# Two batches share the converted weights of the first layer, in a new order of its tiles

## The chip, the cores and the metric

The kernel runs on one core of one Trainium2 chip. The metric is the device time of one execution in microseconds (us). TensorE (PE in the profile) does the matmuls, VectorE (DVE) and ScalarE (ACT) the elementwise work, GpSimd (POOL) some small work and some transfers, SyncE (SP) issues most transfers.

## The reference

An attention of 4 batches, 12 heads, 448 positions and 64 columns per head, with q and k normalized, feeds two layers of weights one after the other:

```
q_n, k_n = rmsnorm(q, g_q), rmsnorm(k, g_k)
attn = softmax(q_n @ k_n^T / 8);  x = attn @ v            # 1792 tokens x 768
h = x @ w_in;  g = h * clip(h + 3, 0, 6) / 6;  x = g @ w_out     # 768 -> 2048 -> 768
h = x @ w2_in; g = max(h, 0)^2;                out = g @ w2_out  # 768 -> 2048 -> 768
```

All in float32 at the outside.

## The kernel before

**Numbers.** A float32 operand of the two layers is split into an upper and a lower float16 half. A product of two operands is three float16 matmuls (upper x upper, upper x lower, lower x upper) into one PSUM tile. A moving operand is 128 x 448: 128 features of one batch.

**Weights of the first layer.** `w_in` is cut into 16 input tiles (128 of the 2048 columns, 768 rows: `INS`), `w_out` into 6 output rows of 128 columns, each in three tiles of 6, 5 and 5 blocks of 128 (`OUTS`, 18 tiles). The weights come in as 64-bit words. `convert` (L962) makes a tile ready for its first use: it loads the raw words into `wr`, rebuilds float32 values in `wf` (`words_of`: the sign L944, a scaled word L927 or L931, the low bytes L937, their union L948, the sum of magnitudes L954 or L951), gets a scale for a family of tiles (two input tiles, or the three of an output row) through a small matmul (`scale_of`), and writes the halves into `ws` (upper L998 or L1001, lower L1005). The halves are also stored to memory (`spill`). The batch that uses a tile first has it `fresh`; every later batch loads it again (`again`, L1131), on SyncE's or GpSimd's queue.

**Units.** `units` (L41) lists the work of the first layer as (batch, layer, tile). Before, a batch's 16 input units come first, then the last 6 output units (two rows) of the batch before it, then its own first 12 output units (four rows). The last 6 of the last batch (`LEFT`) come later, among the second layer's work. `unit` (L1192) issues a unit's matmuls (L1217): an input unit takes 6 blocks x 3 = 18 matmuls and needs the batch's six x tiles (one for each pair of heads), an output row takes 16 blocks x 3 = 48 and needs the 16 tiles of g. A finished input unit goes through the gate (L1249 on ScalarE, L1252 on VectorE) into a raw tile `gr`, which is then split into halves `g` by a factor d (upper L1281 or L1284, lower L1287). The factor (`factors`, L1258) needs the magnitudes of all 16 input tiles, so no g can be split before the last input tile is converted. A finished output row goes to `yr` and to memory (`kept`).

**Attention.** `attention` (L630) does one pair of heads of one batch: scores (L755), the row maximum (L764), the exponential (L709), a transpose (on TensorE at L719 for batch 0 and five of batch 1's pairs, by a transposing transfer `pt` for the others) and the product with v (L823, L842), then the halves of x (L859 to L870).

**Second layer.** `sums` (L1040) converts its weights (`wr_in`, `wr_out`, `wq`, `wc`, `spill_i`, `spill_o`); its matmuls are at L1471 (input) and L1561 (output), with operands loaded as `wi` and `wo`.

**What sets the order.** Every piece of work is a `Task` with a key (its due time, in units), one or two engines that may do it with a cost, tasks that it waits for, and the buffers it uses. `Plan.order` (L200) plays this through and writes each engine's instructions out in the order that results; on the chip every engine takes its own list in that order. Keys come from the position of a unit in the list (`pos`), from `STEPS` and `SCALE` for attention, from `FROM`, `EVERY` and `SOON` for the second layer's weights, from `LOOK0` and `LOOK` for the conversions and reloads; two long tables (`LATER`, `EARLIER`) move single tasks and buffers. Buffers come in classes: "H" (x, gr, g, yr and others) has 48, "w" (wf, ws, wc) has 8 (L140).

Of the kernel before, what the change touches and what calls it, by code (L numbers as in the profile page):

```python
# [60 lines left out]
FROM, EVERY, SOON = 80.22859998528665, (4.041588453004579, 3.7237456628771537), 8.562933226270134  # L61
YLEAD = 12.522739408787375
# [8 lines left out]
    (-247.48221047888984, -394.5979975821401, -98.4527970272032, -242.42713432233748, -222.88569014639836, -217.12283909562356),  # L71
    (-59.661346379600985, -85.02395686962647, 7.106072067009842, 16.896302439366927, -24.194647662679873, 15.416178359589999),
    (43.66694725987674, 32.553603037054934, 46.34866310324863, 49.82797377644987, 49.208523452314246, 51.17752208559789),
    (35.30617020359621, 38.97394296166319, 65.5895982637515, 168.80800044783174, 66.02963739277855, 73.89482410210749),
# [1591 lines left out]
```

## Time and profile before

| | |
|---|---|
| runs | 1115.54, 1122.12, 1120.02 us |
| median | 1120.02 us |
| profiled execution | 1112.35 us, of which the span is 1110.6 us |
| mean granted clock of TensorE | 0.989 |
| TensorE matmuls, busy | 1043.4 us (94%), 5957 instructions |
| VectorE, busy | 887.0 us (80%), 1971 instructions |
| ScalarE, busy | 759.5 us (68%), 1527 instructions |
| transfers | 243.00 MB, mean 219 GB/s |

The span runs from the first to the last instruction of the profiled execution. Busy times are sums over the whole span; the stages have different limits. PEclk is the clock that TensorE was granted as a share of 2.4 GHz, and it has two levels, 2.4 and 1.2 GHz, so 0.95 over a stretch means that a tenth of it ran at the lower level.

### The profile page before, as it was taken

The numbers are of one execution on the slowest core, as the hardware profiler recorded it, in microseconds if no ns is written. First come the engines' busy times: TensorE is split into PE (matmuls) and PEld (weight loads), VectorE is DVE, ScalarE is ACT, GpSimd is POOL, SyncE is SP. The second block draws the span as 40 slices with busy tenths as digits, with TensorE's granted clock in tenths as the row PEclk, the third lists the DMA queues.
The fourth block names the chain that finished last, engine by engine and source line by source line (L and its number), as shares of the span: only waits on it lengthen the run. The fifth ranks groups of instructions, "written<-read, shape, count | busy, mean of one in ns | idle before, by whom it ended". The sixth has DMA issues, their size and how long they took to land.

```text
span 1110.6 us, 17566 instructions
## 1 busy us (share of the span) xinstructions
PE 1043.4 (94%) x5957; PEld 526.5 (47%) x5957; DVE 887.0 (80%) x1971; ACT 759.5 (68%) x1527; POOL 129.6 (12%) x225
## 2 busy tenths in 40 slices
PE   1789999899999999999999999989999999999998
PEld 0445544445444444444555445544445555555554
DVE  7999999997899998999388989796799952128930
ACT  2899989996689666877276767686766645555520
POOL 4411311202221223320000000000000000000000
PEclk9899999899999999999999999999999999999999
DMA  9756578599899999997998898797856664434343
GB/s 297 185 163 163 194 217 239 178 259 240 246 260 192 227 266 261 233 237 179 296 333 277 303 324 319 247 282 245 255 172 213 211 200 116 121 102 134 106 155 106
DMA packets 232313, 243.00 MB, mean 219 GB/s; under 512 B 144608, under 2 KB 188128, under 8 KB 232224
## 3 DMA queue, kind: packets, MB, share of 16 engines
q1 hardware_dynamic: 228576, 225.00, 70.5%
q0 software_dynamic: 3648, 16.88, 5.2%
q8 instruction: 47, 0.77, 0.3%
q14 instruction: 42, 0.34, 0.1%
HBM read 162.76 MB, written 45.61 MB: 188 GB/s over the span
## 4 chain that ended last, share of the span: by engine, by line
PE 59%; DVE 16%; DMA 14%; ACT 8%; issue 2%; SPq 1%; POOL 0%; DVEq 0%; ACTq 0%
PE m L1217 21%; PE mo_0A L1561 3%; PE ps_s L755 3%; PE mo_1A L1561 3%; PE mo_2A L1561 3%; PE ps_a L842 2%; PE ps_a L823 2%; DMA spill_o<-wc_out 2%; DVE ps_s L764 2%; PE ps_s L719 2%; DMA wr<-in_w1o_dram 2%; PE mo_1C L1561 2%; PE mo_2C L1561 2%; PE mo_0C L1561 2%; DMA wi<-spill_i 1%
## 5 line engine op out<-in xcount | busy, mean ns | idle before, releaser
L1217 PEld LDWEIGHTS <-ws 128*128 128x128 f16 x2304 | 217.6, 98 | 222.0 <-issue 24.3
L1217 PE MATMUL m<-g,ws 128*128 128x448 f16 x1152 | 235.5, 355 | 7.3 <-DMA ws<-spill 3.0
L1217 PE MATMUL m<-x,ws 128*128 128x448 f16 x1152 | 233.1, 353 | 0.0
L1471 PEld LDWEIGHTS <-wi 128*128 128x128 f16 x1008 | 98.6, 98 | 98.6 <-DMA wi<-spill_i 5.2
L1561 PEld LDWEIGHTS <-wo 128*128 128x128 f16 x1008 | 98.4, 98 | 92.0 <-DMA wo<-spill_o 0.8
L764 DVE CUSTOM_DVE_ANT_0 ps_s<-ps_s,nought,esc 128x448 f32<-128x448 f32 x168 | 113.4, 684 | 6.7 <-PE ps_s L755 6.6
L709 ACT ACTIVATE e<-ps_s,nm 128x448 f32<-128x448 f32 x168 | 106.6, 637 | 16.1 <-DVE nm L764 9.9
L1508 ACT ACTIVATE go<-gq,g_s 128x448 f16<-128x448 f32 x105 | 62.4, 657 | 35.9 <-DVE gq L1524 13.8
L755 PE MATMUL ps_s<-T 64*128 64x448 f16 (+1 forms) x576 | 75.1, 370 | 2.6 <-DMA T<-src 2.6
L1514 DVE SCALAR_TENSOR_TENSOR go<-gq,g_s,go 128x448 f16<-128x448 f32 x112 | 71.0, 681 | 3.6 <-ACT go L1508 3.5
L719 PE MATMUL ps_s<-eye,e 128*112 128x128 f32 x308 | 50.6, 296 | 14.6 <-ACT e L709 14.5
L783 DVE SCALAR_TENSOR_TENSOR p<-e,su,p 128x448 f16<-128x448 f32 x91 | 59.5, 680 | 5.2 <-ACT p L777 4.9
L777 ACT ACTIVATE p<-e,su 128x448 f16<-128x448 f32 x77 | 48.8, 662 | 17.8 <-DMA pt_5B<-p 4.2
L541 POOL TENSOR_TENSOR rs<-ss,mhalf 128x14 f32<-128x14 f32 x21 | 57.8, 2753 | 1.8
L1249 ACT ACTIVATE t<-m,half,six 128x448 f32<-128x448 f32 x64 | 46.0, 720 | 15.1 <-PE m L1217 14.9
L1487 ACT ACTIVATE gq<-gq 128x448 f32<-128x448 f32 x60 | 34.2, 570 | 27.4 <-DVE gq L1416 25.1
L719 PEld LDWEIGHTS ps_s<-eye,e 128*112 128x112 f32 x308 | 35.7, 141 | 34.8 <-ACT e L709 24.5
L1027 ACT ACTIVATE wc_in<-wq_in,w_in_s 128x384 f16<-128x384 f32 (+1 forms) x43 | 27.6, 651 | 23.4 <-DMA spill_i<-wc_in 8.3
L755 PEld LDWEIGHTS <-T 64*128 64x128 f16 (+1 forms) x576 | 22.1, 99 | 42.6 <-issue 33.5
L1287 DVE SCALAR_TENSOR_TENSOR g<-gr,d,g 128x448 f16<-128x448 f32 x64 | 42.0, 678 | 0.4 <-ACT g L1281 0.3
L1561 PE MATMUL mo_0A<-go,wo 128*128 128x448 f16 x192 | 41.6, 352 | 0.0
L1561 PE MATMUL mo_1A<-go,wo 128*128 128x448 f16 x192 | 41.5, 352 | 0.0
(312 smaller groups left out, 1907.0 us busy)
## 6 DMA issues: line engine op xcount, KB each, us to landing
wi<-spill_i SPq DMA_DIRECT2D x48, 384.0 KB, 3.5
ws<-spill SPq DMA_DIRECT2D x47, 384.0 KB, 5.3
wo<-spill_o SPq DMA_DIRECT2D x42, 384.0 KB, 3.4
wr<-in_w1i_dram SPq DMA_DIRECT2D x16, 768.0 KB, 4.3
wr_in<-in_w2i_dram SPq DMA_DIRECT2D x16, 768.0 KB, 6.8
spill_i<-wc_in SPq DMA_DIRECT2D x24, 384.0 KB, 4.0
wr_out<-in_w2o_dram SPq DMA_DIRECT2D x12, 768.0 KB, 6.7
ws<-spill SPq DMA_DIRECT2D x28, 320.0 KB, 5.5
```

The lines of the kernel that those rows point to most:

```text
L541: nc.gpsimd.tensor_tensor(r, ss, mhalf, op=ALU.pow)
L709: nc.scalar.activation(tl(ve)[:, r % 2], tl(vps)[:, 0:S], AF.Exp, bias=sums["nm"][:, r:r + 1], scale=-1.0, accum_out=sums["su"][:, r:r + 1])
L719: nc.tensor.transpose(o[:, c], tl(ve)[:, r % 2, c * VR:(c + 1) * VR], eye)
L755: nc.tensor.matmul(tl(vpss[x])[at:at + z - a, 0:S], T[e, q0 + a:q0 + z], T[e, k0:k0 + S], start=(i == 0), stop=(i == 2))
L764: nc.vector.tensor_tensor_reduce(x, x, nought.to_broadcast([P, S]), esc, 3e38, ALU.add, ALU.min, sums["nm"][:, r:r + 1])
L777: nc.scalar.activation(tl(vp)[:, r % 2, 0], tl(ve)[:, r % 2], AF.Copy, scale=sums["su"][:, r:r + 1])
L783: nc.vector.scalar_tensor_tensor(tl(vp)[:, r % 2, 1], tl(ve)[:, r % 2], sums["su"][:, r:r + 1], tl(vp)[:, r % 2, 0], op0=ALU.mult, op1=ALU ...
L1217: nc.tensor.matmul(tl(vph)[:, 0:S], w[:, wa, k], tl(rhs[k])[:, xa], start=(first_ and k == 0 and c == 0), stop=(last and k == nf - 1 and c ...
L1471: nc.tensor.matmul(tl(vph)[:, 0:S], w[:, wa, k0 + k], tl(vo)[:, to, xa], start=(starts and k == 0 and x == 0), stop=(k == KH - 1 and x == ...
L1508: nc.scalar.activation(tl(vo)[:, 0], tl(v_), AF.Copy, scale=up)
L1514: nc.vector.scalar_tensor_tensor(tl(vo)[:, 1], tl(v_), up, tl(vo)[:, 0], op0=ALU.mult, op1=ALU.subtract)
L1561: nc.tensor.matmul(tl(vph)[:, 0:S], w[:, g, wa, kk], tl(ops[y])[:, xa], start=(starts and k0 + k + y == 0 and z == 0), stop=(k0 + k + y == ...
```

## The change

- `units` makes groups of batches: (0, 1), (2), (3). In the group of two, batch 0 takes its input tiles 0 to 11 alone; then tiles 12 to 15 are taken by batch 0 and batch 1 in turn; then batch 1 takes its tiles 0 to 11; then the first four output rows are taken row by row, three units of batch 0 and three of batch 1; then the last two rows of batch 0. The last two rows of batch 1 come after batch 2's inputs, as before.
- `unit` keeps a converted tile in its `ws` buffer for both batches where they share it (input tiles 12 to 15 and the first twelve output tiles). Batch 1's tables (`own`) are made as those of batch 0.
- x may take 12 buffers (10 before), gr 32 (17 before).
- For batches 2 and 3 the factor d goes into the gate: steeper slope and shift in L1249, d as the bound in L1252, and the split becomes a plain copy and a subtraction.
- Costs of some tasks in the plan are changed, a table `WAYS` fixes the engine of single tasks, and all numbers that set keys (`FROM`, `EVERY`, `SOON`, `STEPS`, `SCALE`, `VMAX`, `LOOK`, `LOOK0`, `LATER`, `EARLIER`) are new.

```diff
+GROUPS = ((0, 1), (2,), (3,))
+SOLO = 12
+ROW = 3
 def units():
-    seq, left = [], None
-    for b in range(B):
-        seq += [(b, 0, i) for i in INS]
-        if left is not None:
-            seq += [(left, 0, i) for i in OUTS[-TAIL:]]
-        left = b
-        seq += [(b, 0, i) for i in OUTS[:-TAIL]]
-    return seq, [(left, 0, i) for i in OUTS[-TAIL:]]
+    seq, left = [], ()
+    def outs(bs, part):
+        return [(b, 0, i) for o in range(0, len(part), ROW) for b in bs for i in part[o:o + ROW]]
+    for bs in GROUPS:
+        solo = SOLO if len(bs) > 1 else 0
+        seq += [(bs[0], 0, i) for i in INS[:solo]]
+        seq += [(b, 0, i) for i in INS[solo:] for b in bs]
+        seq += [(b, 0, i) for b in bs[1:] for i in INS[:solo]]
+        seq += outs(left, OUTS[-TAIL:])
+        left = bs[-1:]
+        seq += outs(bs, OUTS[:-TAIL]) + outs(bs[:-1], OUTS[-TAIL:])
+    return seq, outs(left, OUTS[-TAIL:])
...
-FROM, EVERY, SOON = 80.22859998528665, (4.041588453004579, 3.7237456628771537), 8.562933226270134
+FROM, EVERY, SOON = 80.97128479369484, (4.113646667126265, 1.3791177970955777), 12.767780398650473
...
-    OWN, SEM, DMA, WAIT = 81, 195, 1300, 297
+    OWN, SEM, DMA, WAIT = 81, 195, 1700, 297
...
-        t = Task(key + 0.001 * LATER.get(len(self.tasks), 0), ways, deps, list(uses), xfer)
+        if len(self.tasks) in WAYS:
+            ways = [ways[WAYS[len(self.tasks)]]]
+        t = Task(key + 0.001 * LATER.get(len(self.tasks), 0), ways, deps, list(uses), xfer, late)
...
-"x": ("H", 10, 10, [P, 2, S], F16),
+"x": ("H", 12, 12, [P, 2, S], F16),
-"gr": ("H", FC + 1, FC + 1, [P, S], F32)
+"gr": ("H", 2 * FC, 2 * FC, [P, S], F32)
...
-        vws, t_w = fresh.pop((m, i)) if (m, i) in fresh else again(m, i, n)
+        vws, t_w = fresh[m, i] if (m, i) in fresh else again(m, i, n)
+        if b == GROUPS[0][-1] or i in OUTS[-TAIL:] or i in INS[:SOLO]:
+            fresh.pop((m, i), None)
...
+        ready = t_tab[b, m][row]
+        if b > 1:
+            d, ready = gfactor[b]
+            steep, shift = slopes[b]
         def g1():
+            if b > 1:
+                nc.scalar.activation(tl(vt), tl(vph)[:, 0:S], AF.Relu, bias=shift[:, row:row + 1], scale=steep[:, row:row + 1])
...
-            nc.vector.scalar_tensor_tensor(tl(vgr), tl(vt), 1.0, tl(vph)[:, 0:S], op0=ALU.min, op1=ALU.mult)
+            nc.vector.scalar_tensor_tensor(tl(vgr), tl(vt), d[:, row:row + 1] if b > 1 else 1.0, tl(vph)[:, 0:S], op0=ALU.min, op1=ALU.mult)
...
+            if b > 1:
+                nc.vector.tensor_tensor(slopes[b][0], six, d, op=ALU.mult)
+                nc.vector.tensor_scalar(slopes[b][1], d, 0.5, None, op0=ALU.mult)
...
+            if b > 1:
+                nc.scalar.copy(tl(vg)[:, 0], tl(vgr))
...
+            if b > 1:
+                nc.vector.tensor_tensor(tl(vg)[:, 1], tl(vgr), tl(vg)[:, 0], op=ALU.subtract)
...
+    for b in GROUPS[0][1:]:
+        own[b] = own[GROUPS[0][0]]
```

## Rows read from the trace of the kernel before

**Rows 1.** Windows: stage, us, then busy time (instructions) per engine, PEclk, DMA share, GB/s.

```profile
30.00:120.00 90.00, 78.60 (x555) 40.86 (x556) 83.85 (x212) 84.57 (x205) 25.25 (x37) 0.94 0.64 176
...
180.00:285.00 105.00, 95.10 (x567) 48.65 (x566) 94.75 (x235) 88.18 (x177) 15.79 (x22) 0.95 0.83 234
285.00:420.00 135.00, 129.37 (x781) 60.76 (x780) 124.56 (x318) 105.20 (x227) 30.83 (x48) 1.00 1.01 234
420.00:600.00 180.00, 179.64 (x1062) 88.35 (x1060) 150.30 (x356) 119.83 (x237) 28.86 (x43) 1.00 0.97 259
600.00:690.00 90.00, 85.66 (x453) 43.94 (x453) 82.24 (x158) 63.73 (x104) 0.71 (x1) 1.00 0.91 314
690.00:840.00 150.00, 142.64 (x742) 72.23 (x741) 124.89 (x246) 104.99 (x212) 0.00 (x0) 0.99 0.75 236
840.00:1110.60 270.60, 266.87 (x1412) 137.85 (x1409) 144.05 (x257) 130.97 (x254) 0.00 (x0) 1.00 0.46 147
```

**Rows 2.** Timeline of PE, 200 to 285: start, us, what, [idle before <- releaser].

```profile
214.03 0.93 PE L1217 MATMUL m<-g,ws 128*128 128x448 f16 x2 [2.41 <-ACT ws L998]
...
215.73 1.68 PE L1217 MATMUL m<-g,ws 128*128 128x448 f16 x4 [0.78 <-DVE ws L1005]
...
265.35 0.55 PE L842 MATMUL ps_a<-pt_4A,v 128*64 128x448 f16 x1 [2.67 <-DMA pt_4A<-p]
```

**Rows 3.** Windows of 10 us, columns as in rows 1.

```profile
210.00:220.00 10.00, 6.18 (x24) 2.34 (x24) 9.99 (x23) 10.00 (x19) 4.50 (x5) 0.69 0.61 231
...
260.00:270.00 10.00, 7.33 (x47) 4.89 (x45) 6.50 (x20) 5.25 (x11) 0.34 (x1) 0.83 1.06 273
270.00:280.00 10.00, 10.00 (x67) 5.29 (x66) 6.06 (x11) 5.04 (x11) 3.43 (x5) 1.00 0.93 271
```

**Rows 4.** Line L1217 up to 282: ns min/median/max, starts; and a dense stretch.

```profile
L1217 PE MATMUL m<-x,ws x297: 351/352/363, 91.5 to 281.0; 128*128 128x448 f16 x149
L1217 PE MATMUL m<-g,ws x173: 351/353/581, 214.0 to 281.9; 128*128 128x448 f16 x173
...
930.00:960.00 30.00, 30.00 (x161) 15.50 (x159) 6.15 (x9) 15.37 (x36) 0.00 (x0) 1.00 0.40 114
```

**Rows 5.** Groups of VectorE by shape: count, busy us, mean ns, idle before.

```profile
L1287 DVE SCALAR_TENSOR_TENSOR g<-gr,d,g 128x448 f16<-128x448 f32 x64 | 42.0, 678 | 0.4 <-ACT g L1281 0.3
...
L1005 DVE SCALAR_TENSOR_TENSOR ws<-wf,w_s,ws 128x768 f16<-128x768 f32 x22 | 22.2, 1010 | 0.1
L948 DVE SCALAR_TENSOR_TENSOR wf<-wr,wf 128x768 int32<-128x768 int32 x22 | 20.9, 951 | 2.4 <-ACT wf L937 2.4
...
L944 DVE TENSOR_SCALAR wf<-wr 128x768 int32<-128x768 int32 x22 | 12.2, 553 | 0.6 <-DMA wr<-in_w1o_dram 0.5
...
L1005 DVE SCALAR_TENSOR_TENSOR ws<-wf,w_s,ws 128x640 f16<-128x640 f32 x12 | 10.6, 879 | 0.1
L948 DVE SCALAR_TENSOR_TENSOR wf<-wr,wf 128x640 int32<-128x640 int32 x12 | 9.8, 818 | 0.0
...
L944 DVE TENSOR_SCALAR wf<-wr 128x640 int32<-128x640 int32 x12 | 5.9, 490 | 0.6 <-DMA wr<-in_w1o_dram 0.6
```

**Rows 6.** Last lower half of tile x before 330; line L948 up to 282.

```profile
L870 DVE TENSOR_TENSOR x<-xr,x x9: 608/620/625, 92.7 to 282.0; 128x448 f16<-128x448 f32 x9
...
L948 DVE SCALAR_TENSOR_TENSOR wf<-wr,wf x28: 803/949/962, 50.3 to 255.1; 128x768 int32<-128x768 int32 x20, 128x640 int32<-128x640 int32 x8
```

**Rows 7.** Tile ws: the reloads by queue.

```profile
L1137 SPq DMA_DIRECT2D ws<-spill x75: 319/527/1112, 263.7 to 813.6; - x75
...
L1137 POOL DMA_DIRECT2D ws<-spill x27: 536/622/797, 243.7 to 659.8; - x27
```

**Rows 8.** PE waits for reloaded weights of the first layer: us, times, longest.

```profile
PE m L1217 <- DMA ws<-spill: 3.0, 2, 2.5
```

**Rows 9.** Groups of VectorE and ScalarE by shape, columns as in rows 5.

```profile
L1252 DVE SCALAR_TENSOR_TENSOR gr<-t,m 128x448 f32<-128x448 f32 x64 | 38.9, 613 | 2.5 <-ACT t L1249 2.4
...
L1281 ACT ACTIVATE g<-gr,d 128x448 f16<-128x448 f32 x59 | 37.3, 664 | 3.8 <-DVE gr L1252 3.8
```

More of the change, by code (lines that the diff above doesn't have):

```diff
@@ L60 @@
 HOME = {"in": "wq", "out": "wq"}
-FROM, EVERY, SOON = 80.22859998528665, (4.041588453004579, 3.7237456628771537), 8.562933226270134
-YLEAD = 12.522739408787375
+FROM, EVERY, SOON = 80.97128479369484, (4.113646667126265, 1.3791177970955777), 12.767780398650473
+YLEAD = 11.075076349190757
 TWIN = 2
@@ L70 @@
 STEPS = (
[L71 to L74, printed above, removed]
-)
-SCALE = (1.0381251219859378, 0.7863150301604104, 0.22475936882802972, 2)
-VMAX = (-186.49537269765818, 67.96134492672827, 95.12270931381782, 147.45138749054064)
+    (-249.71595147789012, -405.5608816675329, -95.52668540219413, -242.85429748667949, -223.63917812762259, -216.49472117550224),
+    (-52.995909324147746, -67.02531224308663, 1.9094299386359455, -32.443268917101975, -42.563992597271614, 15.968080462503766),
+    (43.07111008686646, 35.18456207596165, 46.933668456418964, 49.34017871705987, 52.748203926989525, 49.57753807512902),
+    (37.03670961299758, 44.82375595315473, 58.48054856474226, 205.19532471372665, 63.13676074126832, 82.89667724351747),
+)
+SCALE = (1.0427758708292183, 1.169586376543425, 0.18151455106987216, 2)
+VMAX = (-247.67086964180754, 109.61906769812103, 25.279610510996037, 121.51481273324103)
 SHORT = {1, 2}
-LOOK = (5.565200799245379, 34.652779519986346)
-LOOK0 = (-6.171934184635691, 5.49429662996903, 1.7586957033249144)
+LOOK = (5.644362158968972, 44.70601227882962)
+LOOK0 = (-11.16374042656427, 5.499655920862086, 1.6746538556513277)
 PARTIAL = ((3, 2, 2, 2), (2, 1, 1, 1), (2, 1, 1, 1), (2, 1, 1, 1))
@@ L88 @@
 LATER, EARLIER = {
[11 rows of a table removed]
-}, {
[36 rows of a table removed]
[15 rows of a table added]
+}, {
[27 rows of a table added]
+}
+WAYS = {
[6 rows of a table added]
 }
@@ L162, with __init__ @@
 class Task:
-    def __init__(self, key, ways, deps, uses, xfer):
-        self.key, self.ways, self.xfer = key, ways, xfer
+    def __init__(self, key, ways, deps, uses, xfer, late):
+        self.key, self.ways, self.xfer, self.late = key, ways, xfer, late
         self.uses = uses
@@ L193, in value, with task @@
         return v
-    def task(self, key, ways, deps=(), uses=(), xfer=0):
-        t = Task(key + 0.001 * LATER.get(len(self.tasks), 0), ways, deps, list(uses), xfer)
+    def task(self, key, ways, deps=(), uses=(), xfer=0, late=DMA):
+        if len(self.tasks) in WAYS:
+            ways = [ways[WAYS[len(self.tasks)]]]
+        t = Task(key + 0.001 * LATER.get(len(self.tasks), 0), ways, deps, list(uses), xfer, late)
         self.tasks.append(t)
@@ L292, in order @@
                     line = max(line, now + dur) + int(1.1 * pick.xfer)
-                    end = line + self.DMA
+                    end = line + pick.late
                 else:
@@ L361, in tile_kernel @@
         "v16": ("A", 2, 3, [P, 2, 2, NV, D], F16), "p16": ("A", 3, 4, [P, 2, 2, S], F16),
-        "xr": ("H", 2, 2, [P, S], F32), "tm": ("H", 1, 2, [P, S], F32), "x": ("H", 10, 10, [P, 2, S], F16),
-        "t": ("H", 2, 2, [P, S], F32), "o": ("H", 2, 2, [P, S], F32), "gr": ("H", FC + 1, FC + 1, [P, S], F32), "g": ("H", 2 * FC, 2 * FC, [P, 2, S], F16),
+        "xr": ("H", 2, 2, [P, S], F32), "tm": ("H", 1, 2, [P, S], F32), "x": ("H", 12, 12, [P, 2, S], F16),
+        "t": ("H", 2, 2, [P, S], F32), "o": ("H", 2, 2, [P, S], F32), "gr": ("H", 2 * FC, 2 * FC, [P, S], F32), "g": ("H", 2 * FC, 2 * FC, [P, 2, S], F16),
         "yr": ("H", KC, KC, [P, S], F32), "y": ("H", KC + 2, KC + 2, [P, 2, S], F16),
@@ L624, in norms @@
             dep = t_his if z[1] == 1 else t_los
-            t_trs.append(task(k0 - (14.6 - .02 * z[0]) * sc, [("SP", 1400, lambda z=z: tr(*z))], dep, [vsrc, vT], xfer=1100))
+            t_trs.append(task(k0 - (14.6 - .02 * z[0]) * sc, [("SP", 1400, lambda z=z: tr(*z))], dep, [vsrc, vT], xfer=1170, late=1300))
         first.append(t_trs[-1])
@@ L794, in ptr @@
                     )
-                t_pt[x[0]].append(task(kk + 2.2 * sc, [("SP", 1260, ptr)], [t_pl], [vp, vpt[x[0]]], xfer=(x[2] - x[1]) * 8))
+                t_pt[x[0]].append(task(kk + 2.2 * sc, [("SP", 1260, ptr)], [t_pl], [vp, vpt[x[0]]], xfer=1200, late=1300))
         kx = k0 + (NT + 4) * sc
@@ L1186, in in_table @@
             deps = [wscale[m, x] for x in sorted({family(i)[0] for i in range(a, z)})]
-            t = plan.task(pos[b, m, a] - 1.5, [("DVE", 140, mul)], [t_ix, *deps])
+            t = plan.task(pos[b, m, a] - 1.5, [("DVE", 260, mul)], [t_ix, *deps])
             for i in range(a, z):
@@ L1199, in unit @@
         if kind == "in":
-            if i == 0:
+            if (b, m) not in tables:
                 t_tab[b, m] = in_table(b, m, n)
@@ L1246, in gate @@
         vt = plan.value("t", f"t_{n}", n + .2)
+        ready = t_tab[b, m][row]
+        if b > 1:
+            d, ready = gfactor[b]
+            steep, shift = slopes[b]
         def g1():
-            nc.scalar.activation(tl(vt), tl(vph)[:, 0:S], AF.Relu, bias=half, scale=six[:, row:row + 1])
+            if b > 1:
+                nc.scalar.activation(tl(vt), tl(vph)[:, 0:S], AF.Relu, bias=shift[:, row:row + 1], scale=steep[:, row:row + 1])
+            else:
+                nc.scalar.activation(tl(vt), tl(vph)[:, 0:S], AF.Relu, bias=half, scale=six[:, row:row + 1])
         def g2():
-            nc.vector.scalar_tensor_tensor(tl(vgr), tl(vt), 1.0, tl(vph)[:, 0:S], op0=ALU.min, op1=ALU.mult)
-        t1 = task(n + .2, [("ACT", act(S, 140), g1)], [t, t_tab[b, m][row]], [vph, vt])
-        t_raw[b, m, row] = task(n + .3, [("DVE", dve2(S), g2)], [t1], [vt, vgr, vph])
+            nc.vector.scalar_tensor_tensor(tl(vgr), tl(vt), d[:, row:row + 1] if b > 1 else 1.0, tl(vph)[:, 0:S], op0=ALU.min, op1=ALU.mult)
+        t1 = task(n + .2, [("ACT", act(S, 140), g1)], [t, ready], [vph, vt])
+        t_raw[b, m, row] = task(n + .3, [("DVE", dve2(S) + (60 if b > 1 else 0), g2)], [t1], [vt, vgr, vph])
         halve_g(b, m, row, n)
@@ L1260, in factors @@
         task = plan.task
-        inv, _ = tables[b, m]
+        inv, six = tables[b, m]
         up, down, t_u, t_d = scale_of(n, f"g{b}_{m}", lambda: wsum, [*t_sums, vscale[b][2]], total=lambda: tops[f"v{b}"])
         d = lasting(FC, f"d{b}")
+        if b > 1:
+            slopes[b] = lasting(FC, f"steep{b}"), lasting(FC, f"shift{b}")
         def prod():
             nc.vector.tensor_scalar(d, inv, up, None, op0=ALU.mult)
-        gfactor[b] = d, task(n, [("DVE", 90, prod)], [t_u, *t_tab[b, m].values()])
+            if b > 1:
+                nc.vector.tensor_tensor(slopes[b][0], six, d, op=ALU.mult)
+                nc.vector.tensor_scalar(slopes[b][1], d, 0.5, None, op0=ALU.mult)
+        gfactor[b] = d, task(n, [("DVE", 330 if b > 1 else 130, prod)], [t_u, *t_tab[b, m].values()])
         gscale[b, m] = down, t_d
-    gfactor = {}
+    gfactor, slopes = {}, {}
     def halve_g(b, m, f, n):
@@ L1280, in hi_a @@
         def hi_a():
-            nc.scalar.activation(tl(vg)[:, 0], tl(vgr), AF.Copy, scale=by)
+            if b > 1:
+                nc.scalar.copy(tl(vg)[:, 0], tl(vgr))
+            else:
+                nc.scalar.activation(tl(vg)[:, 0], tl(vgr), AF.Copy, scale=by)
         def hi_v():
-            nc.vector.tensor_scalar(tl(vg)[:, 0], tl(vgr), by, None, op0=ALU.mult)
+            if b > 1:
+                nc.vector.tensor_copy(tl(vg)[:, 0], tl(vgr))
+            else:
+                nc.vector.tensor_scalar(tl(vg)[:, 0], tl(vgr), by, None, op0=ALU.mult)
         def lo():
-            nc.vector.scalar_tensor_tensor(tl(vg)[:, 1], tl(vgr), by, tl(vg)[:, 0], op0=ALU.mult, op1=ALU.subtract)
-        t3 = task(n + .6, [("ACT", act(S, 90), hi_a), ("DVE", dve1(S) + 60, hi_v)], [t_s, t_raw[b, m, f]], [vgr, vg])
-        gdone[b, m, f] = task(n + .61, [("DVE", dve2(S) + 60, lo)], [t3], [vgr, vg])
+            if b > 1:
+                nc.vector.tensor_tensor(tl(vg)[:, 1], tl(vgr), tl(vg)[:, 0], op=ALU.subtract)
+            else:
+                nc.vector.scalar_tensor_tensor(tl(vg)[:, 1], tl(vgr), by, tl(vg)[:, 0], op0=ALU.mult, op1=ALU.subtract)
+        own_ = 0 if b > 1 else 1
+        t3 = task(n + .6, [("ACT", act(S, 90 * own_), hi_a), ("DVE", dve1(S) + 70 + 50 * own_, hi_v)], [t_s, t_raw[b, m, f]], [vgr, vg])
+        gdone[b, m, f] = task(n + .61, [("DVE", dve2(S) + 60 * own_, lo)], [t3], [vgr, vg])
     gscale, yscale = {}, {}
@@ L1457, in mul @@
                 nc.vector.tensor_scalar(inv[:, q:q + 1], iw2i[:, q:q + 1], down, None, op0=ALU.mult)
-            t_c = task(at[1] - 1, [("DVE", 75, mul)], [t_d, wscale_i[q]])
+            t_c = task(at[1] - 1, [("DVE", 130, mul)], [t_d, wscale_i[q]])
             def cells(p, vph, starts, wait, q=q, at=at, ws=ws):
```

95 rows, old and new, of tables (TTR, WAYS) are left out of this document.

## The prediction, written before the changed kernel ran

> **What bounds the kernel now.** I first cut the span into stages [rows 1]. The sum is made against the profiled execution, whose own time is 1112.35 us (span 1110.6 plus 1.75 around it); the median of the three runs, 1120.02, is 1.0069 times that, and I scale by this at the end. The change adds and removes no matmul, so it can win only time in which TensorE stands idle or runs at half its clock. From 840 us on it idles 3.7 us in 270 and is the bound. Before that: 30 to 120, idle 11.4 and clock 0.94 (a loss of 0.06 x 90 = 5.4); 180 to 285, idle 9.9 and clock 0.95 (another 5.2), 15.1 in all; 285 to 420, idle 5.6; 600 to 840, idle 4.3 + 7.4 and clock 0.99 over the last 150 us (1.5). VectorE is busy 94.75 of 105 us and 124.56 of 135 in the two stages where batches 0 and 1 pass through the first layer, ScalarE 88.18 and 105.20: work has to be ready for TensorE, and these two make it. From 420 to 600 VectorE has 30 us to spare.
>
> In 180 to 285 the waits show why. At 214.03 TensorE waits 2.41 us, at 215.73 another 0.78, for halved output tiles of weights: the first output row of batch 0 is due while its three tiles are still being converted. At 265.35 it waits 2.67 us for a transpose of batch 1's attention [rows 2]. After both the granted clock drops to the lower level for a while: 0.69 over 210 to 220, 0.83 over 260 to 270 [rows 3]. The other waits of the stage, 9.9 - 5.9 = 4.0 us, are smaller ones of the softmax and the scales.
>
> **The change, part by part.** (1) The new order of the units. One output row is 48 matmuls, and a matmul takes 30 / 161 = 0.186 us in a dense stretch [rows 4]: 8.9 us for TensorE per batch. Converting its three tiles costs VectorE 2.51 us (768 columns: 0.553 + 0.951 + 1.010) and twice 2.19 (640 columns: 0.490 + 0.818 + 0.879), 6.9 us [rows 5], beside attention on the same engine. Now each converted row of the first four feeds two batches, 17.9 us, and twelve input tiles of batch 1, 216 matmuls or 40 us that need only reloaded weights, stand between batch 0's inputs and the first output row. So the 3.2 us at 214 to 216, and the 0.31 x 10 = 3.1 us of clock behind them, should go: what they wait for is due some 50 us of TensorE later.
>
> The price is that batch 1's attention is due sooner. Unit 13 is batch 1's input tile 12 and needs all six of its x tiles; the last of them is begun at 282.0 now [rows 6], done at 282.6. By 282 TensorE has issued 297 + 173 = 470 matmuls of the first layer [rows 4]; in the new order only 13 units x 18 = 234 stand ahead of unit 13. The 236 that go behind it are 44.0 us; without the 15.1 us lost in this stage TensorE would come to unit 13 at 282.6 - 44.0 - 15.1 = 223.5. When is x ready? VectorE can leave until later: the twelve output tiles converted by then, 28 tiles less 16 input ones [rows 6] (4 x 2.51 + 8 x 2.19 = 27.6), sixteen lower halves of batch 0's g (16 x 0.678 = 10.8) and input tiles 13 to 15 (3 x 2.51 = 7.5), 45.9 us [rows 5]. That puts x at 236.7; if VectorE's idle time of 3.5 + 3.9 us in 260 to 280 [rows 3], behind the late transpose, is filled too, at 229.3. So TensorE waits 13.2 or 5.8 us at unit 13 where it loses 15.1 now: a gain of 1.9 to 9.3 us. The ends: -15.1 if attention is laid out early enough to be no wait at all, +16 for the third rival. I take **-8**, near the upper gain, since that idle time is a latency of attention which other work can cover in the new order, less 1.3 for a stretch at the lower clock like the one after 265 (0.17 x 10 = 1.7).
>
> (2) Sixteen of the 102 reloads fall away (75 from SyncE, 27 from GpSimd [rows 7]): batch 1's input tiles 12 to 15 and its first twelve output tiles. TensorE waits for a reload twice in the run, 3.0 us in all [rows 8], and batches 2 and 3 still reload as before: by itself 0. The cover is attention's other work; without it the price is again a few waits like the 2.67 at 265. In 285 to 420 the DMA share is 1.01, and 16 fewer transfers, with conversion spread out, should ease the late transposes there. Of the 5.6 us idle I take **-2**; ends -5.6 and +5.
>
> (3) Shared output tiles now stay in their buffers over six units instead of three. Three held tiles, three raw ones of the next row and two new halves fill the class of eight exactly; a conversion that is late by this queues on VectorE behind an unready buffer, and TensorE after it. Row against row there is 17.9 us for 6.9 us of VectorE work: 0, end +2. The raw g take up to 32 of the 48 buffers instead of 17, x up to 12: 32 g and 12 x are 44, as today when one batch's tail stands behind the next batch's inputs: 0.
>
> (4) Batches 2 and 3 take the factor d into the gate. Thirty-two minimum-and-multiply steps get a column operand for a constant (from 0.613 towards 0.678, +2.1 us on VectorE), thirty-two lower halves lose one (0.678 to 0.620, -1.9), the upper halves on ScalarE too (0.664 now) [rows 5, 6, 9], and four small products of some 0.2 us come in. Most of this lies between 420 and 600, where VectorE idles a sixth of the time [rows 1]: 0; without that cover +1.
>
> (5) The order laid out anew. Conversion of the second layer's output tiles comes in steps of 1.38 units instead of 3.72 and with a longer lead (12.8 for 8.6). The waits it could remove lie in 600 to 840: 11.7 us idle and 1.5 of clock [rows 1]. The trace cannot show the new order; with no waits -13, with as many again +13; a first layer that ends 10 us sooner makes these due sooner as well. I take **-3**, a quarter. The start, 30 to 120, is attention and the first conversions in both orders: 0, ends -5 and +5.
>
> Sum: -8 - 2 - 3 = -13 us, 1112.35 - 13 = 1099.35, times 1.0069: **1107 us**, 1.2% faster.
>
> **The rivals.** A measurement of this kernel can tell about 0.5% from no change, so faster means under 1114.4, slower over 1125.6.
>
> *VectorE is the bound and the stall only moves.* For it: VectorE is busy 90 to 92% in both stages and its work is the same. TensorE then waits 13.2 us at unit 13 and the gain is 1.9 us; with nothing from the rest 1110.4, or 1118. The same comes out if the new due times leave the output conversions where they are: then the change doesn't do what it says. Against it: the halves and tiles that it defers are not due for 50 us, and 30 us of VectorE are free after 420. 0.20.
>
> *Larger gain.* All idle time and clock of 180 to 420 go (15.1 + 5.6), and 11.7 us of 600 to 840: 1112.35 - 32.4 = 1079.9, or 1087. It needs x ready at 223. 0.10.
>
> *Slower: the stall at unit 13 is longer.* Only the twelve output conversions move out of the way of batch 1's attention, the g halves and the three input tiles stay ahead of it: x at 282.6 - 27.6 = 255, and TensorE, there at 223.5, stands 31.5 us instead of losing 15.1, with one more stretch at the lower clock (1.7): +18, less the 5 of the other parts, 1125.5, or 1133. It decides once x is ready after 223.5 + 15.1 + 5 = 243.6. For it: TensorE takes its matmuls in the order laid out; at 265 it sat through 2.67 us with output rows of batch 0 still unfinished (173 of 192 matmuls issued by 282) [rows 2, 4], and here everything, batch 0's tiles 13 to 15 too, stands behind one x. Against it: 45.9 us of work can move and 7.4 us of idle time can be filled, and 39 in all are enough. 0.17. The Trainium skill (TensorE: Matmul & The Clock Gate, Step-by-step: what each phase is for) states the same rule, that matmuls stay in program order and only weight loads are pulled ahead; by it work behind the late x can't fill the wait, which gives this rival's 1133 where x is at 255. The trace agrees as far as the 2.67 us at 265 goes.
>
> **How the numbers follow.** The forecast holds 0.53, the larger gain 0.10, the moved stall 0.20, the slower case 0.17. The range leaves out the slower case and the far end of the larger gain: from 1090 to 1124. Faster 0.63, same 0.20, slower 0.17.
>
> **What would show it.** Right: no wait for halved output tiles near batch 0's first output row, which begins after 576 first-layer matmuls; last x of batch 1 before 240; one wait of 5 to 10 us ahead of batch 1's first matmul; 86 reloads; idle plus lost clock of TensorE between 180 and 420 down from 20.7 us to about 11. Wrong: TensorE idle over 20 us ahead of unit 13, or the gain of the first layer given back between 600 and 840 in waits for the second layer's weights.

## The result, and the profile after

The changed kernel takes 1103.47 us in the median of four runs (1098.19 to 1110.14), the kernel before, beside it, 1119.56 us (1115.54 to 1122.12): a ratio of 0.9866, 95% interval 0.9825 to 0.9908. The forecast was 1107 us, 1.2% faster; it is 1.3%. The profiled execution took 1103.33 us (span 1101.6), 9.0 less than that of before. TensorE's busy time is the same, 1043.2 for 1043.4 us, so the gain is idle time, 67.2 to 58.4 us.

The windows by stage, columns as in [rows 1]:

```profile
30.00:120.00 90.00, 79.79 (x554) 41.36 (x554) 83.73 (x216) 82.33 (x199) 27.68 (x38) 0.94 0.64 168
...
180.00:285.00 105.00, 97.01 (x608) 46.27 (x608) 102.27 (x277) 91.35 (x196) 22.00 (x32) 0.97 0.78 191
285.00:420.00 135.00, 132.96 (x780) 63.26 (x775) 125.54 (x308) 108.89 (x216) 28.58 (x38) 1.00 1.03 249
420.00:600.00 180.00, 179.26 (x1048) 87.31 (x1046) 145.37 (x341) 107.05 (x205) 21.90 (x33) 1.00 0.94 250
600.00:690.00 90.00, 88.57 (x467) 45.32 (x465) 81.87 (x162) 63.89 (x107) 1.08 (x2) 1.00 0.89 308
690.00:840.00 150.00, 143.95 (x747) 72.78 (x745) 129.78 (x265) 106.36 (x209) 0.71 (x1) 0.99 0.79 254
840.00:1101.60 261.60, 257.69 (x1363) 133.15 (x1361) 138.52 (x249) 123.81 (x238) 0.00 (x0) 1.00 0.44 141
```

Idle plus lost clock, worked out as in the prediction (a low clock while TensorE stands idle counts twice in it, so it is an upper figure), is 8.0 + 3.2 = 11.2 us in 180 to 285 (before 15.1), 2.0 in 285 to 420 (5.6), and 1.4 + 6.1 + 1.5 = 9.0 in 600 to 840 (13.2). The stage from 30 to 120 gives 1.2. There is one profile of the kernel before, so its own spread by stage is not known.

TensorE's timeline from 214 to 262 and, for the last line, from 415 to 440 answers to [rows 2]:

```profile
216.38 0.38 PE L858 MATMUL ps_a<-pt_4A,v 128*64 128x448 f16 x1 [3.17 <-DMA pt_4A<-p]
...
222.80 0.35 PE L1235 MATMUL m<-x,ws 128*128 128x448 f16 x1 [2.12 <-ACT x L875]
223.77 2.03 PE L1235 MATMUL m<-x,ws 128*128 128x448 f16 x5 [0.63 <-DVE x L886]
227.96 0.65 PE L735 MATMUL ps_s<-eye,e 128*112 128x128 f32 x4 [0.48 <-ACT e L725]
233.44 1.14 PE L825 MATMUL ps_r<-eye,su 128*64 128x128 f32 x16 [0.21 <-DVE su L711]
240.22 0.54 PE L1235 MATMUL m<-x,ws 128*128 128x448 f16 x2 [0.24 <-DVE x L886]
...
421.98 0.93 PE L1235 MATMUL m<-g,ws 128*128 128x448 f16 x4 [0.50 <-DVE ws L1021]
```

The 2.41 and 0.78 us for halved output tiles are gone; the only wait of that kind is the 0.50 at 421.98. In their place batch 1's attention costs six waits between 213 and 241, 6.85 us together, the longest again for a transposed tile. The clock falls behind them as it did before: 0.83 and 0.82 in two windows of 10 us, against 0.69 and 0.83 in [rows 3].

```profile
210.00:220.00 10.00, 6.79 (x42) 3.28 (x43) 9.90 (x26) 8.19 (x15) 0.00 (x0) 0.83 1.11 247
220.00:230.00 10.00, 6.78 (x37) 3.28 (x33) 9.32 (x30) 7.61 (x17) 3.67 (x6) 0.82 0.23 72
```

First-layer matmuls on x (all of batches 0 and 1; up to 240 us alone), the last lower half of x, and the matmuls on g, columns as in [rows 4]:

```profile
L1235 PE MATMUL m<-x,ws x576: 349/352/577, 105.3 to 313.4; 128*128 128x448 f16 x192
...
L1235 PE MATMUL m<-x,ws x268: 349/352/577, 105.3 to 239.6; 128*128 128x448 f16 x134
...
L886 DVE TENSOR_TENSOR x<-xr,x x9: 615/620/626, 90.3 to 239.5; 128x448 f16<-128x448 f32 x9
...
L1235 PE MATMUL m<-g,ws x1152: 351/352/364, 313.5 to 813.0; 128*128 128x448 f16 x192
```

The last x is begun at 239.5, done at 240.1 (before 282.6, [rows 6]). The first output row begins right behind the 576th matmul on x. By 239.6 TensorE has issued 268 matmuls, 34 more than the 234 that stand ahead of unit 13 in the list. Reloads are 68 + 18 = 86 for 102 [rows 7], and TensorE waits 0.7 us for them, not 3.0 [rows 8] (last line: us, times, longest):

```profile
L1153 SPq DMA_DIRECT2D ws<-spill x68: 319/524/1210, 212.6 to 795.3; - x68
...
L1153 POOL DMA_DIRECT2D ws<-spill x18: 536/546/812, 196.8 to 782.0; - x18
...
PE m L1235 <- DMA ws<-spill: 0.7, 2, 0.5
```

Both of those waits of the kernel before lay between 600 and 840, and so did its longest wait for a reloaded tile of the second layer, which is gone too:

```profile
PE mi_5A L1471 <- DMA wi<-spill_i: 3.1, 1, 3.1
```

### The profile page after: what moved, and what is told of

Same layout as the page of the kernel before. It is cut to its first block, busy times and chain, and to the rows that moved or that the text cites. A ratio compares the mean times of both kernels' runs of the same rounds, so it can differ in the third digit from the quotient of the medians.

```text
span 1101.6 us, 17547 instructions
## 1 busy us (share of the span) xinstructions
PE 1043.2 (95%) x5957; PEld 524.2 (48%) x5957; DVE 889.7 (81%) x2018; ACT 748.8 (68%) x1496; POOL 129.1 (12%) x220
## 4 chain that ended last, share of the span: by engine, by line
PE 56%; DVE 23%; DMA 11%; ACT 6%; issue 3%; POOL 1%; SPq 0%; DVEq 0%; ACTq 0%
PE m L1235 20%; PE mo_1A L1603 3%; PE mo_0A L1603 3%; PE mo_2A L1603 3%; DVE ps_s L780 3%; DMA spill_i<-wc_in 3%; PE ps_s L771 3%; PE ps_a L839 2%; PE ps_a L858 2%; PE ps_s L735 2%; DMA qk<-in_qk_dram 2%; PE mo_2C L1603 2%; DVE wc_in L1051 2%; PE mo_1C L1603 2%; DMA spill_o<-wc_out 2%
## 5 line engine op out<-in xcount | busy, mean ns | idle before, releaser
L1235 PE MATMUL m<-g,ws 128*128 128x448 f16 x1152 | 230.8, 353 | 0.8 <-DVE ws L1021 0.5
L1550 ACT ACTIVATE go<-gq,g_s 128x448 f16<-128x448 f32 x98 | 59.1, 659 | 38.5 <-DVE gq L1566 19.9
L793 ACT ACTIVATE p<-e,su 128x448 f16<-128x448 f32 x71 | 45.1, 662 | 11.0 <-DVE src L622 6.7
L1529 ACT ACTIVATE gq<-gq 128x448 f32<-128x448 f32 x54 | 30.8, 571 | 25.0 <-DVE gq L1458 23.4
L1603 PE MATMUL mo_2A<-go,wo 128*128 128x448 f16 x192 | 41.5, 352 | 0.0
L1153 POOL DMA_DIRECT2D ws<-spill x18 | 10.9, 608 | 242.9 <-DMA wr_out<-in_w2o_dram 118.8
L1408 ACT ACTIVATE yo<-yu,y_s 128x448 f16<-128x448 f32 x39 | 24.9, 661 | 19.0 <-DVE yu L1426 14.0
```

What stands on the lines that cost most here:

```text
L793: nc.scalar.activation(tl(vp)[:, r % 2, 0], tl(ve)[:, r % 2], AF.Copy, scale=sums["su"][:, r:r + 1])
L1235: nc.tensor.matmul(tl(vph)[:, 0:S], w[:, wa, k], tl(rhs[k])[:, xa], start=(first_ and k == 0 and c == 0), stop=(last and k == nf - 1 and c ...
L1550: nc.scalar.activation(tl(vo)[:, 0], tl(v_), AF.Copy, scale=up)
L1603: nc.tensor.matmul(tl(vph)[:, 0:S], w[:, g, wa, kk], tl(ops[y])[:, xa], start=(starts and k0 + k + y == 0 and z == 0), stop=(k0 + k + y == ...
```

## The experiments

The forecast's theory is that **the order of units** and its due times give the gain. Its first rival: **the layout**, that is the new keys and tables, gives it whatever the order. Its second: **fewer transfers** give it. Two finer ones came up on the way: whether the doubled matmuls of an output row pay or its later due time, and whether the amount of VectorE's work sets the time of batch 1's x. The tables `LATER`, `EARLIER` and `WAYS` name tasks by number and hold for one order only; "no tables" sets them to nothing, after which a line of the code stands 52 lines higher.

**1 to 4. Order and keys, two by two, without tables.**

```diff
-LATER, EARLIER = {
...
+LATER, EARLIER, WAYS = {}, {}, {}
```

and for the old order `GROUPS = ((0,), (1,), (2,), (3,))`, for the old keys the numbers of the kernel before.

> The changed kernel with its three tables of single moves (LATER, EARLIER, WAYS) emptied; units, keys and costs as changed. Theory A (the order of the units itself brings the gain): against the same kernel with the old order of units (e2) it is 4 to 12 us faster, with less idle time of TensorE up to the end of batch 1's outputs. Theory B (the gain is in the newly laid out tables, the order only moves the stall): within 4 us of e2 or slower. By both it is slower than the changed kernel, by 10 to 60 us, since the tables were made for it.

> As e1, but with each batch its own group: the old order of units, nothing shared, the new keys and costs. Theory A: 4 to 12 us slower than e1, with waits for halved output tiles in batch 0's output rows like the 3.2 us of the kernel before. Theory B: within 4 us of e1 or faster.

> As e1, with the keys of the kernel before (FROM, EVERY, SOON, YLEAD, STEPS, SCALE, VMAX, LOOK, LOOK0), no tables: the new order of units under the old due times. Theory A: 4 to 12 us faster than e4; batch 1's attention may come late by these keys, then a wait of up to 15 us stands ahead of its first input unit and the gain is less. Theory B: not faster than e4; new keys against old (e1 against e3) make more than 5 us.

> As e3, with the old order of units: the kernel before without its tables, with the factor in the gate and the new costs. Theory A: 4 to 12 us slower than e3. Theory B: within 4 us of e3 or faster. By both slower than the kernel before, by 10 to 60 us.

Measured, against 1118.82 us for the kernel before: new order and new keys 1135.35 us (1133.48 to 1138.67; ratio 1.0146, 1.0098 to 1.0194), old order and new keys 1146.03 (1144.10 to 1149.14; 1.0240, 1.0191 to 1.0290), new order and old keys 1148.30 (1.0264, 1.0208 to 1.0321), old order and old keys 1151.64 (1.0291, 1.0239 to 1.0344). So the order is worth 10.7 us at the new keys (4 to 12 were expected of the forecast's theory) and 3.3 at the old ones, where the intervals overlap. The changed kernel's tables are worth 1135.35 - 1103.47 = 31.9 us, those of the kernel before 1151.64 - 1118.82 = 32.8: large, but alike on both sides, so having tables is not the difference. The keys are worth 13 us in the new order and 5.6 in the old one. From corner to corner, old order and old keys to new order and new keys, it is 1151.64 - 1135.35 = 16.3 us without tables, as much as the whole gain with them.

The trace of the old order (experiment 2), TensorE's timeline, then windows, then its longest waits from 420 to 600 (us, times, longest), shows the waits of [rows 2] again, and where its loss is:

```profile
230.36 0.76 PE L1183 MATMUL m<-g,ws 128*128 128x448 f16 x2 [1.86 <-ACT ws L962]
231.64 3.20 PE L1183 MATMUL m<-g,ws 128*128 128x448 f16 x10 [0.53 <-DVE ws L969]
```

```profile
180.00:285.00 105.00, 98.36 (x597) 48.54 (x598) 103.23 (x264) 97.50 (x200) 19.53 (x27) 0.97 0.79 236
...
420.00:600.00 180.00, 158.14 (x897) 76.63 (x891) 125.25 (x296) 96.23 (x200) 27.52 (x42) 0.94 0.92 212
```

```profile
PE ps_s L719 <- ACT e L673: 8.9, 3, 3.6
PE w_in_p L394 <- DVE w_in_s L388: 7.9, 1, 7.9
```

The same views of the new order (experiment 1):

```profile
227.17 1.10 PE L683 MATMUL ps_s<-eye,e 128*112 128x128 f32 x4 [8.64 <-ACT e L673]
...
304.23 2.40 PE L1183 MATMUL m<-x,ws 128*128 128x448 f16 x6 [5.90 <-ACT e L673]
```

```profile
180.00:285.00 105.00, 89.96 (x577) 45.01 (x576) 96.48 (x266) 86.56 (x189) 20.94 (x30) 0.95 0.73 172
...
420.00:600.00 180.00, 173.07 (x1036) 83.36 (x1035) 140.01 (x338) 116.55 (x238) 32.15 (x48) 1.00 1.01 239
```

The new order takes the waits for output tiles away, and waits for batch 1's attention come instead: in 180 to 285 it idles 15.0 us, the old order 6.6. Its gain is later, in 420 to 600: 6.9 us idle at full clock against 21.9 at 0.94. There the old order waits for the attention of later batches and for the second layer's weights. So without tables the order of units does bring a gain, but not in the stage where the forecast put it. The stage does not carry over to the kernels with tables: there the kernel before idles 0.4 us from 420 to 600 [rows 1] and has nothing to give.

**5 and 6. The changed kernel again, and with the old gate.** Number 5 emits the same instructions through rewritten bookkeeping; number 6 keeps order and plan, and takes the factor out of the gate again:

```diff
-            if b > 1:
+            if b > 9:
...
-            nc.vector.scalar_tensor_tensor(tl(vgr), tl(vt), d[:, row:row + 1] if b > 1 else 1.0, tl(vph)[:, 0:S], op0=ALU.min, op1=ALU.mult)
+            nc.vector.scalar_tensor_tensor(tl(vgr), tl(vt), 1.0, tl(vph)[:, 0:S], op0=ALU.min, op1=ALU.mult)
```

> The changed kernel with the same instructions in the same order, as the control for the other runs on this chip. Both theories: the ratio to the kernel before is 0.987 within its interval.

> The changed kernel in the same plan and order, but batches 2 and 3 use the old instructions in gate and split (constant bound, factor d in both halves). Theory A (part 4 of the prediction, 0): the same time as the control within 2 us; minimum-and-multiply of batches 2 and 3 back to 0.613 us, lower halves back to 0.678, upper halves on ScalarE back to 0.664, no new wait of TensorE. Theory C (ScalarE's shorter upper halves carry some of the gain): 3 to 6 us slower than the control, with waits of TensorE for g between 440 and 660.

1106.70 us (1098.23 to 1110.13; ratio 0.9869, 0.9820 to 0.9917) and 1104.65 us (0.9875, 0.9822 to 0.9928): the gate is worth nothing that shows. Its instructions cost what the prediction said. The changed kernel's groups, columns as in [rows 5]:

```profile
L1278 DVE SCALAR_TENSOR_TENSOR gr<-t,d,m 128x448 f32<-128x448 f32 x32 | 21.7, 677 | 0.8 <-ACT t L1273 0.7
...
L1326 DVE TENSOR_TENSOR g<-gr,g 128x448 f16<-128x448 f32 x32 | 19.6, 619 | 0.7 <-ACT g L1314 0.7
```

Both also give further profiles of the same order. Windows of number 5, then of number 6:

```profile
180.00:285.00 105.00, 95.64 (x600) 45.96 (x599) 100.87 (x274) 89.87 (x190) 22.30 (x32) 0.95 0.80 186
285.00:420.00 135.00, 132.53 (x776) 63.01 (x775) 125.57 (x306) 109.58 (x216) 28.81 (x38) 1.00 1.04 246
420.00:600.00 180.00, 176.05 (x1022) 84.78 (x1021) 140.95 (x339) 100.66 (x196) 21.39 (x33) 0.99 0.94 241
600.00:840.00 240.00, 231.70 (x1216) 118.04 (x1215) 211.26 (x426) 174.73 (x322) 1.80 (x3) 1.00 0.84 277
```

```profile
180.00:285.00 105.00, 97.51 (x603) 46.06 (x599) 101.35 (x276) 90.77 (x193) 22.30 (x32) 0.93 0.80 191
285.00:420.00 135.00, 132.37 (x774) 62.95 (x772) 125.50 (x312) 108.90 (x215) 28.69 (x38) 1.00 1.01 247
...
600.00:840.00 240.00, 230.38 (x1209) 117.43 (x1208) 211.19 (x425) 170.15 (x313) 1.79 (x3) 1.00 0.83 274
```

In 180 to 285 idle plus lost clock is 9.4 + 5.2 = 14.6 and 7.5 + 7.3 = 14.8 here, 11.2 in the first profile, 15.1 before. In 285 to 420 it is 2.5 and 2.6 (2.0; 5.6 before), in 600 to 840 8.3 and 9.6 (9.0; 13.2 before). The gains of these two stages repeat; that of 180 to 285 is between 0.3 and 3.9 us. But number 5 loses 3.95 + 1.8 = 5.75 us from 420 to 600, where the kernel before loses 0.4 and the other two profiles 0.7 and nothing, so not all that is gained behind 285 is kept in every execution.

**7 and 9. Sixteen transfers put back.** Each shared unit of batch 1 copies its weights from `spill` to a place that nothing reads. Number 7 makes them tasks of the plan; number 9 issues them from SyncE where the unit's first matmul stands, and leaves every other engine's list as it is (the edit of number 9):

```diff
+                if not a and b == 1 and (i in INS[SOLO:] or i in OUTS[:-TAIL]):
+                    nc.sync.dma_start(spare[m * UH + i][:, :, 0:nf * P], spill[m * UH + i][:, :, 0:nf * P])
```

> The changed kernel with the sixteen transfers that sharing removes put back as bare load: at each of batch 1's units on a shared tile SyncE moves the tile's stored halves to a place that nothing reads. Theory A (part 2: by itself 0): within 3 us of the control, no wait of TensorE behind these transfers. Theory D (the transfers removed are the gain, by the late transposes of 285 to 420): 4 to 8 us slower than the control, with waits of TensorE for transposes or reloads in 240 to 400 that the control does not have.

> Sixteen bare transfers as in e7, but written into the finished order: every engine's own instructions are those of the control in the same order, and SyncE issues one transfer more ahead of each of batch 1's units on a shared tile. Theory A (the transfers by themselves are worth 0; e7's loss came from the order, which the plan drew up anew around the added work): ratio to the kernel before 0.987 as the control, within 0.4%. Theory D (the transfers are the gain): 0.995 or more, with waits of TensorE for transposes between 240 and 400.

Number 7 took 1152.00 us (1.0281, 1.0237 to 1.0325), but it says nothing of transfers: with sixteen more tasks the plan drew another order, for TensorE too, and the tables were made for the old one. Number 9 took 1120.91 us in twelve runs (1114.72 to 1127.05; 1.0022, 0.9989 to 1.0055), which is the whole gain of the change: in this order the transfers are not worth the 0 of the prediction's part (2). Its transfers, the waits of TensorE that are new or longer (timeline), and its windows:

```profile
L1234 SPq DMA_DIRECT2D spare<-spill x16: 486/582/1462, 209.5 to 430.1; - x16
```

```profile
270.59 0.36 PE L772 MATMUL ps_s<-T 64*128 64x448 f16 x2 [1.46 <-DMA T<-src]
272.52 0.55 PE L772 MATMUL ps_s<-T 64*128 64x448 f16 x4 [1.56 <-DMA T<-src]
...
380.23 0.58 PE L457 MATMUL w_p<-w_s,ones 1*128 1x2 f32 x2 [4.19 <-DVE w_s L454]
...
437.41 1.27 PE L772 MATMUL ps_s<-T 64*128 64x448 f16 x5 [5.92 <-ACT e L726]
```

```profile
180.00:285.00 105.00, 91.00 (x571) 43.00 (x570) 96.74 (x262) 86.70 (x183) 22.07 (x32) 0.95 0.83 186
285.00:420.00 135.00, 130.71 (x748) 62.13 (x747) 122.30 (x295) 106.67 (x209) 26.80 (x35) 0.97 1.05 268
```

The sixteen themselves land in 5.3 us in the median. But transposing transfers land late. The issues of `pt_4B` (attention's transpose) from 362 to 374 here, then in the changed kernel, then those of T (q and k, turned by a transfer) from 420 to 440 here (number issued, median us to landing):

```profile
pt_4B<-p SPq DMA_TRANSPOSE x2, 11.2
```

```profile
pt_4B<-p SPq DMA_TRANSPOSE x2, 7.8
```

```profile
T<-src SPq DMA_TRANSPOSE x2, 12.7
```

The other three profiles of this order without the copies (numbers 5, 6 and 10) have 7.9, 7.4 and 7.3 us for the first pair, so its 11.2 goes with the copies; VectorE idled 5.47 us for it up to 377.53, shortly ahead of the 4.19 at 380.23. The T pair shows less: the 12.7 us end just ahead of the 5.92 at 437.41, and the exponential on ScalarE that this matmul waits for had itself idled 9.36 us for T, but the like pair takes 7.2 us in the changed kernel and 8.9, 6.6 and 10.5 in numbers 5, 6 and 10, with a wait of 0.27, 2.73, 0.27 and 4.22 us at the same matmul. Idle plus lost clock is 19.2 us from 180 to 285 and 8.4 from 285 to 420, 27.6 in all, where the four profiles without the copies have 11.9 to 17.4. These copies also write to memory, as the reloads don't, and each takes SyncE 0.58 us in the median to issue, so their price need not be that of the reloads; whether the reading, the writing or the place in SyncE's list makes the transposes late was not tried.

**8 and 11. Batch 1 reloads its first twelve output tiles,** behind batch 0's four rows (`ROW = 12`), with the tables and without.

```diff
-ROW = 3
+ROW = 12
...
-        vws, t_w = fresh[m, i] if (m, i) in fresh else again(m, i, n)
+        keep = i in INS[12:]
+        if b == 0 or b == 1 and keep:
+            vws, t_w = fresh[m, i]
+        else:
...
+            vws, t_w = again(m, i, n)
```

> The changed kernel with the first four output rows taken batch by batch (ROW = 12): batch 0's twelve units, then batch 1's, which load the halves again; input tiles 12 to 15 stay shared, output tiles still follow both batches' inputs. Theory A (the gain is that output tiles are due after both batches' inputs, and each converted row feeds two batches): 3 to 8 us slower than the control, with waits of TensorE for halved output tiles in batch 0's four rows (8.9 us of matmuls for 6.9 us of VectorE per row); if the later due time alone is enough, within 3 us. Theory B (all is in the tables): over 8 us slower, spread over the later stages.

> e1 (new order, no tables) with the first four output rows taken batch by batch; batch 1 loads those twelve tiles again. Both sides without tables, so the plan is drawn up anew on both. Theory A1 (the doubled matmuls per converted row carry the gain): 5 to 11 us slower than e1, near e2. Theory A2 (the later due time of the output tiles carries it): within 4 us of e1.

Number 8 took 1141.63 us (1.0195, 1.0145 to 1.0246), near the level without tables: it has the flaw of number 7, and decides nothing. Number 11 took 1129.95 us in ten runs (1.0095, 1.0062 to 1.0128), not slower than number 1 (1.0146, 1.0098 to 1.0194) but 5.4 us less, with intervals that overlap a little. So, without tables, twelve reloads cost nothing where the plan is drawn around them, and that each converted row feeds two batches is not what pays: what is left of the order theory is that output rows come due behind both batches' inputs.

**12. Batch 1's inputs behind all of batch 0's** (`SOLO = 16`, four input tiles reloaded, no tables).

```diff
-SOLO = 12
+SOLO = 16
```

> e1 with all sixteen input tiles of batch 0 ahead of batch 1's (SOLO = 16), output rows shared as in e1; batch 1's first unit is 16 instead of 13, 54 matmuls or 10 us later. If the wait at unit 13 costs what the trace shows: up to 8 us faster than e1, with TensorE's wait ahead of batch 1's first unit gone. If sharing the last four input tiles is part of the gain: 2 to 6 us slower than e1.

1141.25 us (1.0198, 1.0152 to 1.0245), 5.9 more than number 1, with intervals that overlap a little. The idle time in 180 to 285 falls to 6.0 us, so the early unit 13 does cost there; more is lost again from 420 to 600 (16.4). Which link ties the two was not tried.

**10. Less work for VectorE ahead of x.** Eleven multiplications of batches 0 and 1 go to GpSimd, in the same order:

```diff
-            nc.vector.tensor_tensor(x, x, gg[:, None, :].to_broadcast([P, NR, D]), op=ALU.mult)
+            eng = nc.gpsimd if j < 2 and (j, p) != (0, 0) else nc.vector
+            eng.tensor_tensor(x, x, gg[:, None, :].to_broadcast([P, NR, D]), op=ALU.mult)
```

> The changed kernel in the same order, with the multiplication by the norm's weights (0.618 us on VectorE each) given to GpSimd for eleven pairs of batches 0 and 1: 6.8 us less work on VectorE before batch 1's last x. Theory E (VectorE's work sets when batch 1's x is ready, as in part 1 of the prediction): x done some 3 to 7 us before 240, TensorE's waits between 210 and 245 shrink from 7 us to 3 or less, and the run is 2 to 6 us faster than the control. Theory F (the wait is a chain of latencies: a transposing transfer, ScalarE, a matmul): x within 2 us of 240, the time as the control, or slower where GpSimd's longer instruction lies on the chain.

1109.07 us (0.9886, 0.9837 to 0.9936): no change. The groups of both engines, then all engines up to the end of the last x, here and in the changed kernel (columns as in [rows 1]):

```profile
L598 POOL TENSOR_TENSOR qk<-qk,gg 128x448 f32<-128x448 f32 x11 | 13.5, 1226 | 15.7 <-DVE qk L593 8.5 <-PE ps_s L772 2.6 <-ACT e L726 2.0
L598 DVE TENSOR_TENSOR qk<-qk,gg 128x448 f32<-128x448 f32 x13 | 8.0, 618 | 0.0
```

```profile
0.00:241.90 241.90, 199.89 (x1306) 103.23 (x1307) 223.22 (x573) 199.61 (x442) 79.17 (x142) 0.96 0.72 193
```

```profile
0.00:240.10 240.10, 196.92 (x1306) 101.61 (x1307) 224.10 (x584) 199.08 (x442) 65.90 (x131) 0.96 0.70 194
```

The eleven should free 11 x 0.618 = 6.8 us of VectorE, but its busy time ahead of the last x falls by 0.9 us only, from 224.1 us with 584 instructions to 223.2 with 573: others of its instructions take longer here. So the experiment made VectorE hardly lighter, and it decides neither way. The last x is begun at 241.3, against 239.5, which both theories would give for a VectorE with as much work as before; that the steps of attention behind each other set this time was not shown. An order drawn anew for the lighter VectorE was not tried.

No kernel of the study is faster than the changed one by more than the intervals.

## Why the prediction was right, step by step

The sum was right, -13 us against -9.0 between the two profiled executions and -16.1 between the medians; its parts were not.

**(1) Order of units, -8: over-sized.** The waits for output tiles went, the first output row came behind 576 matmuls, and x was ready before 243.6, so the slower rival's condition was not met. But idle plus lost clock of the stage fell by 0.3 to 3.9 us over three profiles. The part that failed is "VectorE can leave until later", 45.9 us: it puts x at 229.3 to 236.7, and x came at 240.1. Unions (one for each converted tile) and lower halves in the changed kernel up to 240, then the kernel before up to its own last x:

```profile
L964 DVE SCALAR_TENSOR_TENSOR wf<-wr,wf 128x768 int32<-128x768 int32 x16 | 15.1, 947 | 0.0
...
L1328 DVE SCALAR_TENSOR_TENSOR g<-gr,d,g 128x448 f16<-128x448 f32 x12 | 7.3, 667 | 0.0
```

```profile
0.00:282.60 282.60, 236.78 (x1503) 122.25 (x1504) 258.57 (x637) 232.99 (x496) 69.18 (x134) 0.96 0.75 217
```

All sixteen input tiles were converted ahead of x, 13 to 15 too, and twelve of batch 0's sixteen lower halves were split; of the prediction's list only the output conversions (27.6 us) and four halves (2.7) had left. In all, VectorE did 224.1 us of work ahead of x, not 258.6, which is 34.5 less, and its idle time fell from 24.0 to 16.0, where up to 7.4 was allowed for: 282.6 - 34.5 - 8.0 = 240.1. The clock term was too small as well: 1.3 taken, though the row that it cites gives 1.7, and 3.2 to 7.3 measured. That TensorE still lost only 6.85 us there, not the 240.1 - 223.5 = 16.6 that this x would give, is another error the other way: not everything stands behind unit 13. The plan laid 34 more matmuls (6.3 us) ahead of the last x, blocks of unit 13 and later units for which x was there. The rule that the slower rival quoted from the Trainium skill (TensorE: Matmul & The Clock Gate, Step-by-step: what each phase is for) agrees with this trace: the 2.12 us at 222.80 is a matmul waiting at its place. The list of units is not that program order; it is only what the order is drawn from. The rival of the stall that only moves is, for this stage, what two of the three profiles show. Of the signs, x stood at its bound (240), the one wait of 5 to 10 us was six of 6.85 together, and idle plus lost clock of 180 to 420 fell to 13.2, 17.1 and 17.4 us in the three profiles, not to about 11.

**(2) Sixteen reloads, "by itself 0" and -2 for the late transposes: the stage of the -2 gave -3.0 to -3.6, the 0 is not general.** Put into a fixed order, sixteen transfers cost some 12 to 14 us (experiment 9 against 10 and 5). The prediction had named the price, "a few waits like the 2.67 at 265", but had not counted the clock behind each and the waits after 420. Without tables, with the plan drawn around them, twelve reloads cost nothing (experiment 11). How much of the measured gain comes from the reloads that fell away stays open.

**(3) Buffers, 0,** and **(4) the gate, 0:** no wait for a buffer shows among the rows above, and experiment 6 holds (4) up; 0.677 and 0.619 us are the sizes that were forecast.

**(5) Order laid out anew, -3 in 600 to 840:** the stage gave -3.6 to -4.9 in three profiles. In the first of them two waits for reloaded tiles make up more than the 4.2 us: 3.0 to 0.7 for the first layer's, which part (2) had put at 0, and 3.1 for the second layer's. No experiment tells whether the new order or the fewer reloads took them away. The start, 0, gave 1.2 in the first profile.

So the gain lies behind 285 more than ahead of it, in each of the three profiles, though each is set against the one profile of the kernel before. That the sum came out is in part luck: a part that was over-sized, two that were under-sized and a division between them that no experiment settles. Experiments 1 and 2 show for one profile each, without tables, that what the order of units brings, it brings from 420 on; that output conversions spread out leave room there for later batches' attention and the second layer's weights is a reading of their waits, not shown. How the 16 us divide between the order and the keys and tables drawn for it is not settled: without tables 3 to 11 us go with the order and 6 to 13 with the keys, and each order's own tables bring 32 to 33.

## What to carry to other kernels

A wait is removed by making its work due behind other work that needs nothing new, and the same move makes something else due sooner; look for the gain in later stages, too, where the freed engine is used. A table of single moves fits one order alone: undo a part of such a change with the emitted order held fixed, or without tables on both sides. When TensorE's place at a stall is estimated from a list of units, count the parts of later units that are ready before it; when a gain rests on work that can be deferred, read from the new order which of it was.
